# Decay sums unsplit in the fp32 stacks, decay rows in fewer partitions, later float32r stacks

## Chip, core and metric

The kernel runs on one core of a Trainium2 chip. The metric is the device time in microseconds (us) of one execution, median over several runs; less is better. Beside the time there is one profiled execution, from which all rows below come.

## What is computed

An attention with a decay, and two feed-forward layers over its output. In short:

```python
q, k, v: (4, 8, 576, 64)   f: (4, 8, 576)            # float32
cum = cumsum(log(clip(f, 1e-4, 1)), axis=-1)         # the decay sums
scores = q @ k^T / 8 + cum[:, :, :, None] - cum[:, :, None, :]   # masked causally
attn = softmax(scores) @ v                           # then (2304, 512)
h = x @ w1_in;  y = (h * tanh(softplus(h))) @ w1_out # 512 -> 2048 -> 512
h = y @ w2_in;  out = (h * cos(h)) @ w2_out          # 512 -> 2048 -> 512
```

The weights come as float64 and are split on the chip into two float32r parts (`split_weights`).

## The kernel before

**Attention.** `attention_units` works through jobs of two heads of one batch. Batch 0 (`CUT_BATCHES`) is cut into 8 jobs: four of the query blocks 0 and 1 (256 tokens), then four of the blocks 2 to 4. The batches 1 to 3 have four jobs each. `whole(jb)` is true for the 8 jobs of batch 0; the score products of these are plain fp32 (line 503), those of the other 12 jobs are sums of two float32r products (line 510).

**The stacks.** A score product takes its operands from a stack, a tile of 128 partitions whose rows 0 to 63 hold q or k, transposed. The decay enters the same product through more rows: where q has -1, k has cum of the key, and where k has 1, q has cum of the query. Before the change each cum stands as two rows, a float32r part hi and the rest lo (`cums`, `cumd`). They lie in partitions 64, 65 (k) and 96, 97 (q). `new_stack` (lines 652 to 660) fills the 32 partitions around them with four memsets: zeros in q[96:128] and k[64:96], always by GpSimd (lines 656, 657), then -1 and 1 (lines 658, 659) by the engine `en`. There are two fp32 stacks `stk0`, `stk1` and two float32r stacks `stkr0`, `stkr1`, used in turn by odd and even jobs. `stk0`, `stk1` and `stkr0` are made before the first job (lines 674 to 679), `stkr1` at its first use, in the place of the fp32 stacks.

**The start.** `decay_tables` loads f, clips it, takes Ln (ScalarE) and the running sum (VectorE scan, line 751), splits it into hi (ScalarE, line 753) and lo (VectorE, line 754). Then the jobs' loads are issued, and `prep_job(0)`: the row DMAs of job 0 from SBUF (line 426, four of them), the two writes of the sums to DRAM (`cumd`, line 434), transposes of q and k on TensorE (line 450) and the copies into the stack: of q the first head by VectorE (line 475), all the others by ScalarE (line 473). Later jobs read their rows from DRAM (line 428, two DMAs each). All DMAs are issued from SyncE's in-order queue.

**Per query block.** `scores` makes the products, a fused add of the mask with a minimum on VectorE (line 553, it reads `maskt` or `mask2`), exp on ScalarE (559); `normalise` scales on GpSimd (573); `transposes` (599, 610) and `av` (635) follow. `make_masks` fills the masks on GpSimd (lines 732 to 742).

**Beside it.** The weights of the first layer are converted piece by piece, one about every second query block: a load (105), two steps on VectorE (124, 125), a scaling on GpSimd (129), VectorE (134), ScalarE (138), GpSimd (139). Its first load is issued behind the write to DRAM marked `marks["cum"]`. After the first four jobs the products x @ w1_in of finished tokens (line 154) are put between the attention's steps; after the attention come the rest of both layers. Within these lists the order on each engine is made by a planner at build time (`schedule_with_timeline_sim=True`), which simulates the engines and issues, of what is ready, what comes first in the program; so instructions may stand in another order than in the text.

Of the kernel before, what the change touches and what calls it, by code (L numbers as in the profile page):

```python
# [9 lines left out]
F32 = mybir.dt.float32  # L10
F32R = mybir.dt.float32r
I32 = mybir.dt.int32
AF = mybir.ActivationFunctionType
ALU = mybir.AluOpType
# [18 lines left out]
def f(ap):  # L33
    return ap.bitcast(F32)
# [3 lines left out]
def tile_attention_two_ffn(  # L38
# [12 lines left out]
    nc = tc.nc  # L51
    B, H, S, D = q.shape
# [15 lines left out]
    dram = ctx.enter_context(tc.tile_pool(name="dram", bufs=1, space=DRAM))  # L68
# [8 lines left out]

    hd = dram.tile([128, NJ, NT], F32, name="hd")
    yd = dram.tile([128, 2, NK, NT], F32, name="yd")
    cumd = dram.tile([B * H, 2, S], F32, name="cumd")  # L80


# [3 lines left out]
    marks, cums = {}, []  # L86
# [268 lines left out]
    def attention_units(p, bank):  # L355
# [11 lines left out]
        def whole(jb):  # L367
            return jobs[jb][0] // NP in CUT_BATCHES
# [47 lines left out]
        def prep_job(jb):  # L416
            if jb >= len(jobs):
                return
            b, hp, qlo, khi, last = span(jb)
            qn, kn = nat.pop(jb)  # L420
            st = stack(jb)
            h0 = b * H + 2 * hp
            for row, x in ((96, 0), (64, 1)) if whole(jb) else ((96, 2), (64, 3)):
                if jb == 0:
                    for y in range(2):
                        nc.sync.dma_start(out=st[row + y : row + y + 1, x], in_=cums[y][h0 : h0 + 2])
                else:
                    nc.sync.dma_start(
                        out=st[row : row + 2, x] if whole(jb) else f(st[row : row + 2, x]),
                        in_=cumd[h0 : h0 + 2].rearrange("h y s -> y h s")  # L430
                    )
            if jb == 0:
                for y in range(2):
                    marks["cum"] = nc.sync.dma_start(out=cumd[:, y], in_=cums[y])
            yield
            cols = []
            for which, src, lo in ((0, qn, qlo), (1, kn, 0)):
                P, C = SPLIT[khi - lo]
                cols += [(which, src, P, C, c) for c in range(C)]
            full, groups = 512, []  # L440
            for x in cols:
                if full + x[2] > 512:
                    groups.append([])
                    full = 0
                groups[-1].append(x + (full,))
                full += x[2]
            for g in groups:
                t = bank()
                for which, src, P, C, c, at in g:
                    nc.tensor.transpose(t[:, at : at + P], src[0:P, c].rearrange("p h d -> p (h d)"), ident[0:P, 0:P])  # L450
                for which, lo in ((0, qlo), (1, 0)):
                    run = [x for x in g if x[0] == which]
                    if not run:
                        continue
                    _, _, P, C, c0, at = run[0]
                    n = len(run)
                    lo_x = 0 if which == 0 else 3
                    lo_r = slice(64, 128) if which == 0 else slice(0, 64)

                    def part(rows, x, j):  # L460
                        if jb == 0:
                            return st[rows, x, j, lo:khi].rearrange("r (p c) -> r c p", c=C)[:, c0 : c0 + n]
                        return st[rows, x, j, lo + c0 * P : lo + (c0 + n) * P]

                    sc = 0.125 if which == 0 else 1.0
                    if whole(jb):
                        for j in range(2):
                            i_ = t[64 * j : 64 * j + 64, at : at + n * P]
                            if jb == 0:
                                i_ = i_.rearrange("r (c p) -> r c p", p=P)  # L470
                            o = part(slice(0, 64), which, j)
                            if which or j:
                                nc.scalar.activation(out=o, in_=i_, func=AF.Copy, scale=sc)
                            else:
                                nc.vector.tensor_scalar(out=o, in0=i_, scalar1=sc, scalar2=None, op0=ALU.mult)
                        continue
                    for j in range(2):
                        i_ = t[64 * j : 64 * j + 64, at : at + n * P]
                        hi = part(slice(0, 64), which, j)
                        nc.scalar.activation(out=hi, in_=i_, func=AF.Copy, scale=sc)  # L480
                        nc.vector.scalar_tensor_tensor(
                            out=part(lo_r, lo_x, j), in0=i_, scalar=sc, in1=f(hi), op0=ALU.mult, op1=ALU.subtract
                        )
                    both = slice(0, 2)
                    dup = (slice(0, 64), 2) if which == 0 else (slice(64, 128), 1)
                    nc.gpsimd.tensor_copy(part(*dup, both), f(part(slice(0, 64), which, both)))
                yield
            if jb:
                load_v(jb + 1)
            load_job(jb + 2)  # L490

        def scores(jb, i):
            st = stack(jb)
# [6 lines left out]
            def product(o, j, c0, c1, first=QS[i], m=r):  # L500
                if whole(jb):
                    at = j * S + first
                    marks["score"] = nc.tensor.matmul(  # L503
                        o, lhsT=st.rearrange("p x j s -> p (x j s)")[0:128, at : at + m],
                        rhs=st[0:128, 1, j, c0:c1], start=True, stop=True,
                    )
                    return
                for x in range(2):
                    at = (4 * x + j) * S + first
                    marks["score"] = nc.tensor.matmul(  # L510
                        o, lhsT=st.rearrange("p x j s -> p (x j s)")[0:128, at : at + m],
                        rhs=st[0:128, 2 * x + 1, j, c0:c1], start=(x == 0), stop=(x == 1),
                    )

            heads = []
            if w == 64:
                t = bank()
# [3 lines left out]
                for j in range(2):  # L521
                    rows = slice(w * j, w * j + w)
                    heads[0].append((t[rows, w * j : w * j + w], 0, w, maskt[rows, S - 128 + w * j : S - 64 + w * j], rows))
            elif r == 64:
                t = bank()[:, 0:w]
# [6 lines left out]
            else:  # L532
                cuts = [(0, w)] if w <= 512 else [(0, w // 2), (w // 2, w)]
                heads = [[], []]
                for c0, c1 in cuts:
                    n = c1 - c0
                    t = None
                    for j in range(2):
                        if t is None or 2 * n > 512:
                            t = bank()  # L540
                        o = t[:, j * n : j * n + n] if 2 * n <= 512 else t[:, 0:n]
# [3 lines left out]
            for j, parts in enumerate(heads):  # L545
                s = p.tile([128, S], F32, tag="s", name="s", bufs=7)
# [105 lines left out]
        def new_stack(pool, name, dt, en):  # L652
            one = dt == F32
            t = pool.tile([128, 2 if one else 4, 2, S], dt, name=name, bufs=1)
            q, k = (t[:, 0], t[:, 1]) if one else (f(t[:, 2]), f(t[:, 3]))
            nc.gpsimd.memset(q[96:128], 0.0)
            nc.gpsimd.memset(k[64:96], 0.0)
            en.memset(q[64:96], -1.0)
            en.memset(k[96:128], 1.0)
            return t  # L660

        def stack(jb):
            key = (whole(jb), jb % 2)
            if key not in stacks:
                if key == (False, late % 2):
                    early.close()
                    pool = late_sb.enter_context(tc.tile_pool(name="stk", bufs=1))
                else:
                    pool = p
                stacks[key] = new_stack(pool, f"stkr{jb % 2}", F32R, nc.gpsimd)  # L670
            return stacks[key]
# [3 lines left out]
        for i in range(2):  # L675
            stacks[True, i] = new_stack(e, f"stk{i}", F32, nc.gpsimd if i else nc.vector)
            if i == 0:
                make_masks()
        stack(late - 1)
        for jb in range(2):  # L680
            load_job(jb)
        load_v(0)
        load_v(1)
        for _ in prep_job(0):
            pass
        prep = None
        M = len(items)
        LT = PAIR_LAG
# [55 lines left out]
    def decay_tables(p):  # L744
        NH = B * H
        ft, cum, one = (p.tile([128, S], F32, tag="s", name="s", bufs=7)[0:NH] for _ in range(3))
        nc.sync.dma_start(out=ft, in_=fg.rearrange("b h s -> (b h) s"))
        nc.vector.tensor_scalar(out=ft, in0=ft, scalar1=1e-4, scalar2=1.0, op0=ALU.max, op1=ALU.min)
        nc.scalar.activation(out=ft, in_=ft, func=AF.Ln)
        nc.gpsimd.memset(one, 1.0)  # L750
        nc.vector.tensor_tensor_scan(out=cum, data0=one, data1=ft, initial=0.0, op0=ALU.mult, op1=ALU.add)
        ch, cl = (x.bitcast(F32R) for x in (ft, one))
        nc.scalar.activation(out=ch, in_=cum, func=AF.Copy)
        nc.vector.tensor_tensor(out=cl, in0=cum, in1=ft, op=ALU.subtract)
        cums.extend((ft, one))

    hidden = [(0, 256), (256, S - 256)] + [(b * S + x, S // 2) for b in range(1, B) for x in (0, S // 2)]
    first = [(0, TH), (TH, TH), (2 * TH, NT % TH)] + [(NT - TH * i, TH) for i in (2, 1)]
# [137 lines left out]
```

## Time and profile before

| | us |
|---|---|
| median of 3 runs (1055.45 to 1059.02) | 1055.91 |
| profiled execution | 1053.56 |
| its span, first to last instruction | 1051.8 |
| TensorE busy in the span | 1011.2 |
| VectorE / ScalarE / GpSimd busy | 598.3 / 537.6 / 236.9 |

Engines in rows: PE is TensorE's matmul, PEld its weight load, DVE VectorE, ACT ScalarE, POOL GpSimd, SP SyncE; SPq is SyncE's queue, whose rows are the time an issue takes there. A name such as L503 is line 503 of the kernel. In a timeline the columns are start, duration (of all in the row), engine, line, operation, out<-in, shape, count, and in brackets the idle time before with what ended it. In a table of stretches each engine has its busy time and (count), then come the granted clock of TensorE as a share of full speed, the DMA engines' share, and GB/s.

### The profile page before, as it was taken

How to read it: one execution, taken by the hardware profiler on the slowest of the kernel's cores; microseconds unless marked ns; L12 is line 12 of the kernel's file. 1: busy time of each engine (PE TensorE's matmuls, PEld its weight loads, DVE VectorE, ACT ScalarE, POOL GpSimd, SP SyncE). 2: the span in 40 equal slices, each digit the busy share in tenths (PEclk: the TensorE clock that was granted, in tenths of full speed). 3: DMA queues.
4: the chain of work that ended last, by engine and by line, in shares of the span. 5: the costliest groups of instructions: out<-in, count | busy, mean ns of one | idle time of the engine just before them, and what ended most of it. 6: DMA issues, size and time to landing. Idle time of an engine off the chain costs nothing.

```text
span 1051.8 us, 16908 instructions
## 1 busy us (share of the span) xinstructions
PE 1011.2 (96%) x5920; PEld 865.8 (82%) x5920; DVE 598.3 (57%) x1402; ACT 537.6 (51%) x1142; POOL 236.9 (23%) x331
## 2 busy tenths in 40 slices
PE   5798899999999999999999999999999999999998
PEld 4586779899999999977778888888888888888897
DVE  5858755666555536746664267766444544454454
ACT  4666746665556536446664465644433333333343
POOL 7647643433323312412120012111000000000000
PEclk9999999999999999999999999999999999999999
DMA  4655423333331138756966365412100300110010
GB/s 118 169 151 123 136 70 95 85 93 89 84 90 60 57 117 277 238 176 196 325 206 223 111 195 177 159 41 71 50 1 1 120 1 1 41 41 1 1 41 21
DMA packets 118361, 111.80 MB, mean 106 GB/s; under 512 B 66564, under 2 KB 87044, under 8 KB 118276
## 3 DMA queue, kind: packets, MB, share of 16 engines
q1 hardware_dynamic: 118276, 110.72, 34.5%
q8 instruction: 47, 0.77, 0.3%
q14 instruction: 38, 0.31, 0.1%
HBM read 77.49 MB, written 33.18 MB: 105 GB/s over the span
## 4 chain that ended last, share of the span: by engine, by line
PE 77%; DMA 8%; DVE 5%; ACT 4%; issue 3%; POOL 3%; SPq 0%; ACTq 0%; POOLq 0%; DVEq 0%
PE h L154 24%; PE acc L257 19%; PE hx L154 9%; DMA hl<-hd 5%; PE s L635 5%; PE acc L249 5%; PE s L610 4%; PE s L510 3%; PE hx L249 2%; PE h L249 2%; PE s L450 2%; PE s L503 2%; DMA raw<-in_moe_w_in_dram 1%; POOL wol L139 1%; DVE gl L319 1%
## 5 line engine op out<-in xcount | busy, mean ns | idle before, releaser
L154 PE MATMUL h<-xb,wih 128*128 128x288 f32 (+2 forms) x848 | 184.2, 305 | 4.0 <-ACT wih L138 2.7
L154 PEld LDWEIGHTS h<-xb,wih 128*128 128x128 f32 x848 | 138.7, 191 | 7.1 <-ACT wih L138 3.2
L154 PE MATMUL h<-xb,wil 128*128 128x288 f32 (+2 forms) x424 | 126.3, 300 | 0.0
L559 ACT ACTIVATE s<-s,mx 128x448 f32<-128x448 f32 (+5 forms) x144 | 83.7, 582 | 68.4 <-DVE mx L553 64.4
L257 PE MATMUL acc<-woh,gh 128*128 128x512 f32 x288 | 112.9, 392 | 0.0
L257 PE MATMUL acc<-woh,gl 128*128 128x512 f32 x288 | 112.3, 391 | 0.0
L257 PE MATMUL acc<-wol,gh 128*128 128x512 f32 x288 | 112.0, 389 | 0.0
L573 POOL TENSOR_SCALAR s<-s,sm 128x448 f32<-128x448 f32 (+5 forms) x144 | 82.8, 588 | 124.4 <-DVE sm L571 63.4
L319 DVE TENSOR_TENSOR gl<-hl,gh 128x512 fp32r<-128x512 f32 x72 | 65.0, 904 | 70.5 <-ACT gh L314 70.4
L154 PE MATMUL hx<-x,wih 128*128 128x512 f32 (+1 forms) x320 | 92.7, 369 | 0.0
L154 PE MATMUL h<-x,wih 128*128 128x512 f32 (+1 forms) x320 | 91.0, 369 | 0.0
L305 ACT ACTIVATE n<-n 128x512 f32<-128x512 f32 (+1 forms) x80 | 47.1, 589 | 85.8 <-DVE n L299 85.6
L139 POOL TENSOR_TENSOR wol<-raw,woh 128x512 fp32r<-128x512 f32 x32 | 45.3, 1416 | 197.6 <-ACT woh L138 174.0
L553 DVE CUSTOM_DVE_ANT_0 s<-s,maskt 128x288 f32<-128x288 f32 (+6 forms) x152 | 63.7, 430 | 45.3 <-PE s L510 24.9
L319 DVE TENSOR_TENSOR gl<-e,gh 128x512 fp32r<-128x512 f32 (+1 forms) x80 | 53.8, 672 | 50.7 <-ACT gh L314 50.5
L154 PEld LDWEIGHTS h<-xb,wil 128*128 128x128 f32 x424 | 79.9, 190 | 1.3 <-issue 0.8
L298 DVE TENSOR_SCALAR n<-e 128x512 f32<-128x512 f32 (+1 forms) x80 | 32.7, 408 | 84.3 <-ACT e L291 83.8
L288 ACT ACTIVATE hl<-hl 128x512 f32<-128x512 f32 x72 | 45.1, 629 | 61.1 <-DMA hl<-hd 59.4
L314 ACT ACTIVATE gh<-e 128x512 fp32r<-128x512 f32 (+1 forms) x80 | 47.1, 588 | 52.3 <-DVE e L310 48.9
L249 PE MATMUL acc<-gl,woh 128*128 128x512 f32 (+1 forms) x192 | 68.5, 358 | 3.3 <-DVE gl L319 3.2
L249 PE MATMUL acc<-gh,wol 128*128 128x512 f32 (+1 forms) x192 | 67.8, 354 | 0.0
L154 PEld LDWEIGHTS h<-x,wih 128*128 128x128 f32 x320 | 58.4, 188 | 11.0
(119 smaller groups left out, 2215.7 us busy)
## 6 DMA issues: line engine op xcount, KB each, us to landing
hl<-hd SPq DMA_DIRECT2D x72, 256.0 KB
raw<-in_moe_w_in_dram SPq DMA_DIRECT2D x32, 512.0 KB
raw<-in_moe_w_out_dram SPq DMA_DIRECT2D x32, 512.0 KB
hd<-hs SPq DMA_DIRECT2D x48, 288.0 KB
yd<-stage SPq DMA_DIRECT2D x32, 256.0 KB
x<-yd SPq DMA_DIRECT2D x32, 256.0 KB
natk<-in_k_dram SPq DMA_DIRECT2D x32, 144.0 KB
out_dram<-stage SPq DMA_DIRECT2D x18, 256.0 KB
```

The source lines that it names most:

```text
L139: nc.gpsimd.tensor_tensor(out=lo[sl], in0=f(high), in1=f(hi[sl]), op=ALU.subtract)
L154: nc.tensor.matmul(o, lhsT=a[wsl], rhs=b[:, kk, :], start=(kk == 0 and i == 0), stop=(kk == NK - 1 and i == 2),)
L249: nc.tensor.matmul(acc[ti][d][:, 0:T], lhsT=a[dsl], rhs=b[:, gs], start=(start and i == 0), stop=(end and i == 2),)
L257: nc.tensor.matmul(acc[ti][m], lhsT=a[:, ms], rhs=b[:, j % 2, :], start=(start and i == 0), stop=(end and i == 2),)
L288: nc.scalar.activation(out=e, in_=e, func=AF.Mish, scale=UNSCALE)
L305: nc.scalar.activation(out=t, in_=t, func=AF.Sin, scale=TWO_PI)
L314: nc.scalar.activation(out=gh, in_=e, func=AF.Copy)
L319: marks["v1"] = nc.vector.tensor_tensor(out=gl, in0=st.pop(n)[0], in1=f(gst[n][0]), op=ALU.subtract)
L553: marks["ttr"] = nc.vector.tensor_tensor_reduce(out=s[rows, c0:c1], in0=o, in1=mk, scale=-1.0, scalar=BIG if prev is None or rows.start el ...
L559: nc.scalar.activation(out=s[:, 0:w], in_=s[:, 0:w], func=AF.Exp, scale=-1.0, bias=mx, accum_out=sm[:, j : j + 1])
L573: nc.gpsimd.tensor_scalar(out=s[:, 0:w], in0=s[:, 0:w], scalar1=sm[:, j : j + 1], scalar2=1.0, op0=ALU.mult, op1=ALU.mult)
L635: pair = nc.tensor.matmul(t[64 * j : 64 * j + 64, c0:width], lhsT=vt[jb][:, c, j], rhs=pt[:, j, c, c0:width], start=(c == 0), stop=(c == n ...
```

## The change

The fp32 stacks take cum itself, one row for k (partition 64) and one for q (partition 65), where hi and lo had been; a new DRAM tensor `cumf` holds it for later jobs. The float32r stacks keep hi and lo, now in partitions 64, 65 (k) and 66, 67 (q). `new_stack` has two memsets, both by `en`, over 2 or 4 partitions; the zero memsets are gone, and the products take 66 partitions (fp32) or 128 and 68 (float32r). The split into hi and lo and its two writes to DRAM come in `decay_parts`, behind `prep_job(0)`. `stkr0` is made at its first use, in `prep_job(8)`. Of job 0, VectorE copies both heads of q, and ScalarE both of k.

```diff
+    cumf = dram.tile([B * H, S], F32, name="cumf")
...
-            for row, x in ((96, 0), (64, 1)) if whole(jb) else ((96, 2), (64, 3)):
-                if jb == 0:
-                    for y in range(2):
-                        nc.sync.dma_start(out=st[row + y : row + y + 1, x], in_=cums[y][h0 : h0 + 2])
-                else:
+            if whole(jb):
+                for row, x in ((64, 1), (65, 0)):
                     nc.sync.dma_start(
-                        out=st[row : row + 2, x] if whole(jb) else f(st[row : row + 2, x]),
-                        in_=cumd[h0 : h0 + 2].rearrange("h y s -> y h s")
+                        out=st[row : row + 1, x], in_=cums[0][h0 : h0 + 2] if jb == 0 else cumf[h0 : h0 + 2]
+                    )
+            else:
+                for row, x in ((64, 3), (66, 2)):
+                    nc.sync.dma_start(
+                        out=f(st[row : row + 2, x]), in_=cumd[h0 : h0 + 2].rearrange("h y s -> y h s")
                     )
             if jb == 0:
-                for y in range(2):
-                    marks["cum"] = nc.sync.dma_start(out=cumd[:, y], in_=cums[y])
+                marks["cum"] = nc.sync.dma_start(out=cumf, in_=cums[0])
...
-                            if which or j:
+                            if which or j and jb:
...
-                        o, lhsT=st.rearrange("p x j s -> p (x j s)")[0:128, at : at + m],
-                        rhs=st[0:128, 1, j, c0:c1], start=True, stop=True,
+                        o, lhsT=st.rearrange("p x j s -> p (x j s)")[0:66, at : at + m],
+                        rhs=st[0:66, 1, j, c0:c1], start=True, stop=True,
...
-                for x in range(2):
+                for x, rows in ((0, 128), (1, 68)):
...
-            nc.gpsimd.memset(q[96:128], 0.0)
-            nc.gpsimd.memset(k[64:96], 0.0)
-            en.memset(q[64:96], -1.0)
-            en.memset(k[96:128], 1.0)
+            rows = slice(64, 66 if one else 68)
+            en.memset(q[rows], -1.0)
+            en.memset(k[rows], 1.0)
...
-        stack(late - 1)
...
         for _ in prep_job(0):
             pass
+        decay_parts()
...
-        ch, cl = (x.bitcast(F32R) for x in (ft, one))
-        nc.scalar.activation(out=ch, in_=cum, func=AF.Copy)
-        nc.vector.tensor_tensor(out=cl, in0=cum, in1=ft, op=ALU.subtract)
-        cums.extend((ft, one))
+        cums.extend((cum, ft, one))
+
+    def decay_parts():
+        cum, hi, lo = cums
+        nc.scalar.activation(out=hi.bitcast(F32R), in_=cum, func=AF.Copy)
+        nc.vector.tensor_tensor(out=lo.bitcast(F32R), in0=cum, in1=hi, op=ALU.subtract)
+        for y, t in enumerate((hi, lo)):
+            nc.sync.dma_start(out=cumd[:, y], in_=t)
```

## Rows read from the trace of the kernel before

**Rows 1.** Table of stretches, the whole span by stage.
```profile
0.00:50.00 50.00, 30.98 (x161) 21.98 (x162) 33.75 (x108) 30.14 (x82) 33.88 (x57) 0.99 0.61 150
...
80.00:143.00 63.00, 53.01 (x401) 42.67 (x399) 51.87 (x159) 43.44 (x113) 44.70 (x63) 0.95 0.46 118
...
200.00:400.00 200.00, 200.00 (x1602) 184.91 (x1602) 108.17 (x396) 112.80 (x303) 60.36 (x116) 1.00 0.31 89
```

**Rows 2.** Timeline of PE, 4 to 19 us.
```profile
11.56 1.20 PE L503 MATMUL s<-stk 128*128 128x128 f32 x4 [5.67 <-DMA stk<-s]
16.46 1.20 PE L503 MATMUL s<-stk 128*128 128x128 f32 x4 [0.66 <-DMA stk<-cumd]
```

**Rows 3.** Timeline of SP's queue, 7 to 15 us.
```profile
6.98 0.47 SPq L411 DMA_DIRECT2D natv<-in_v_dram  x1
7.58 2.73 SPq L426 DMA_DIRECT2D stk<-s  x4
10.37 0.86 SPq L434 DMA_DIRECT2D cumd<-s  x2
11.32 1.40 SPq L388 DMA_DIRECT2D natq<-in_q_dram  x2
...
14.24 0.68 SPq L428 DMA_DIRECT2D stk<-cumd  x2
```

**Rows 4.** Timelines of DVE and ACT, 0 to 15 us.
```profile
5.20 1.35 DVE L751 TENSOR_TENSOR_SCAN s<-s 32x576 f32<-32x576 f32 x1 [0.82 <-POOL mask L737]
6.48 0.58 DVE L475 TENSOR_SCALAR stk<-s 64x256 f32<-64x256 f32 x1
...
14.18 0.27 DVE L553 CUSTOM_DVE_ANT_0 s<-s,maskt 128x128 f32<-128x128 f32 x1
...
6.58 0.68 ACT L753 ACTIVATE s<-s 32x576 fp32r<-32x576 f32 x1 [1.49 <-DVE s L751]
7.29 1.90 ACT L473 ACTIVATE stk<-s 64x256 f32<-64x256 f32 x3
```

**Rows 5.** Timeline of POOL, 0 to 60 us.
```profile
1.53 1.06 POOL L656 MEMSET stk<- 32x1152 f32 x1
...
12.64 1.05 POOL L659 MEMSET stkr<- 32x1152 f32 x1
13.76 0.29 POOL L733 TENSOR_SCALAR_AFFINE_SELECT maskt<-maskt 128x128 f32<-128x128 f32 x1
```

**Rows 6.** Weight loads of all 128 rows and of 96, by shape, whole span.
```profile
L610 PEld LDWEIGHTS s<-ident,s 128*128 128x128 f32 x432 | 51.4, 145 | 3.4 <-DVE stkr L481 1.5 <-POOL s L573 1.0 <-issue 0.2
L450 PEld LDWEIGHTS s<-ident,natk 96*128 96x128 f32 x96 | 10.9, 146 | 0.2 <-issue 0.2
```

**Rows 7.** Timelines of POOL, DVE and PE around the making of stkr1.
```profile
98.30 1.05 POOL L659 MEMSET stkr<- 32x1152 f32 x1
99.44 0.71 POOL L129 TENSOR_SCALAR raw<-raw 128x512 f32<-128x512 f32 x1
...
94.73 0.43 DVE L124 TENSOR_SCALAR raw<-raw 128x512 int32<-128x512 int32 x1 [1.16 <-DMA raw<-in_moe_w_in_dram]
...
98.51 1.13 DVE L124 TENSOR_SCALAR raw<-raw 128x512 int32<-128x512 int32 x1
...
103.94 0.91 PE L635 MATMUL s<-p,natv 128*64 128x64 f32 x12 [2.58 <-DVE p L594]
```

**Rows 8.** Table of stretches, two in which the granted clock is at half.
```profile
104.00:110.00 6.00, 6.00 (x38) 5.88 (x39) 2.42 (x10) 4.19 (x12) 3.45 (x4) 0.50 0.33 100
50.00:54.00 4.00, 4.00 (x17) 3.59 (x18) 2.33 (x2) 0.86 (x2) 3.61 (x5) 0.50 0.18 32
```

**Rows 9.** Timelines of PE and of SP's queue, two single rows.
```profile
49.87 0.87 PE L599 MATMUL s<-ident,s 128*128 128x128 f32 x3 [4.15 <-DVE xb L648]
...
37.57 0.65 SPq L428 DMA_DIRECT2D stkr<-cumd  x2
```

**Rows 10.** Table of stretches, the four us around the start of stkr1's memsets.
```profile
92.00:96.00 4.00, 3.17 (x21) 2.56 (x20) 2.40 (x7) 1.76 (x5) 3.88 (x7) 1.00 0.94 288
```

More of the change, by code (lines that the diff above doesn't have):

```diff
@@ L503, in product @@
                     marks["score"] = nc.tensor.matmul(
-                        o, lhsT=st.rearrange("p x j s -> p (x j s)")[0:128, at : at + m],
-                        rhs=st[0:128, 1, j, c0:c1], start=True, stop=True,
+                        o, lhsT=st.rearrange("p x j s -> p (x j s)")[0:66, at : at + m],
+                        rhs=st[0:66, 1, j, c0:c1], start=True, stop=True,
                     )
                     return
-                for x in range(2):
+                for x, rows in ((0, 128), (1, 68)):
                     at = (4 * x + j) * S + first
                     marks["score"] = nc.tensor.matmul(
-                        o, lhsT=st.rearrange("p x j s -> p (x j s)")[0:128, at : at + m],
-                        rhs=st[0:128, 2 * x + 1, j, c0:c1], start=(x == 0), stop=(x == 1),
+                        o, lhsT=st.rearrange("p x j s -> p (x j s)")[0:rows, at : at + m],
+                        rhs=st[0:rows, 2 * x + 1, j, c0:c1], start=(x == 0), stop=(x == 1),
                     )
```

## The prediction

> **What bounds the kernel now.** I read the table of stretches first, then the timelines of the start, engine by engine, then the waits of PE. PE is busy 200 us of 200 between 200 and 400 us [rows 1], and nearly so to the end, so nothing that the change does to other engines can count there. Only two stages have room: the first 50 us, where PE works 30.98 us, and 80 to 143 us, where it idles 10 us [rows 1]. What is gained in them arrives at the end if the same instructions follow in the same order, since all later PE work is then simply started sooner.
>
> In the start PE first waits 5.67 us for the decay rows of job 0 [rows 2]. Those were the four issues on SP's queue from 7.58 to 10.31, and the last landed about 1.25 us after its issue (11.56 - 10.31) [rows 2, 3]. DVE's first masked minimum comes only at 14.18, 2 us after the first products [rows 2, 4]: it needs the mask, whose select stood behind all memsets of POOL and ran at 13.76 [rows 5]. The rows of job 1, issued at 14.24, are the next wall (PE at 16.46 waits for them) [rows 2, 3].
>
> **The change part by part.** The sum is made against the profiled execution, 1053.56 us with a span of 1051.8; the median is 2.35 us (0.2%) above it. I take differences and put them on the median, 1055.91.
>
> *First wall, rows of job 0.* cum is there when the scan ends, 5.20 + 1.35 = 6.55 [rows 4]. SP's queue is busy with loads of v until 6.98 + 0.47 = 7.45, which the planner finds ready and earlier in the program, so the first row issue stays at about 7.58 [rows 3]. Two issues in place of four cost 2.73 / 2 = 1.37 instead of 2.73: the last leaves at 8.95, lands at 10.2, and PE starts about 1.4 us sooner. If the v loads were passed, 0.9 us more. The copies don't hold it: ScalarE has two of 1.90 / 3 = 0.63 us, done by 7.29 + 1.27 = 8.56 even if they start no sooner than now; VectorE two of 0.58 from 6.48, done by 7.7 [rows 4].
>
> *Mask wall.* POOL loses eight of ten memsets of 1.05 us (two of stk0, two of stk1, four of stkr0) ahead of the select [rows 5], so the mask is ready before 8 and DVE starts when the first products are there, about 10.8 instead of 14.18: 3.4 us. That is the most that the start can gain.
>
> *Second wall, rows of job 1.* On SP's queue, from 7.58 to 14.24, stand four row issues (2.73), two writes (0.86) and four loads [rows 3]. After: two rows (1.37), one write of cumf (0.43), the loads, and the two moved writes of `decay_parts` (0.86), which come before job 1's rows in the program. Saved: 3.59 - 2.66 = 0.93 us; 1.8 if the moved writes slip behind. PE's second job, at 16.46, comes so much sooner. The split itself (0.68 on ScalarE [rows 4], a little more on VectorE) moves into time in which both idle until 14 us; without that cover it would cost about 1.4.
>
> So the start gains between 0.9 us (SP decides) and 3.4 (the mask decides). The next stage hangs on PE's and SP's walls and on DVE's, so I take a value nearer the lower end, 1.6. Late next is DVE, whose in-order queue carries both softmax and weight conversion.
>
> *Matmuls with 66 or 68 rows.* The trace has no such score product. A weight load of 96 rows takes 146 ns, one of 128 rows 145 [rows 6]: I take nothing. Bounds: 1 ns either way on each score load, and these are fewer than the 432 of the row: 0.4 us either way.
>
> *stkr1.* Two memsets fewer when it is made: POOL's L129 at 99.44, which follows the four directly, can start up to 2.1 us sooner [rows 7]. One DVE step beside the last memset, L124 at 98.51, takes 1.13 us instead of 0.43 [rows 7]. PE idles 2.58 us shortly behind, until 103.94 [rows 7]. Bounds 0 and 2.1 us; the chain runs through VectorE's and ScalarE's steps too, so I take 0.8.
>
> That DVE step is weighed against the Trainium skill: "SBUF — State Buffer", section "Who interferes with whom", says that VectorE's two-port forms and a GpSimd instruction exclude each other for a whole instruction. The row agrees (1.13 against 0.43); by the rule the memsets put at a new place cost VectorE up to their full length there, 2.1 us for two, which would eat the 0.8 and 1.3 more. It speaks against the later stkr0.
>
> *stkr0 at its first use.* Two memsets of 1.05 us move from the start to `prep_job(8)`, ahead of that job's row issues, which SP reached at 37.57 [rows 9], long before job 8 computes. I expect the planner to put them into one of POOL's free spells before 50 us (16 us are free there [rows 1]): cost 0; bound 2.1 if in the way.
>
> Sum: -1.6 - 0.8 + 0 = -2.4, so 1055.91 - 2.4 = 1053.5. Bounds: -0.9 + 2.1 = +1.2 and -3.4 - 2.1 = -5.5.
>
> **The rivals.** *A stretch of slow clock goes too.* The granted clock is 0.95 to 1.00 on average in the stages [rows 1] (2.4 GHz is the full level), but 0.50 (1.2 GHz) in 50 to 54 and in 104 to 110 us [rows 8], after PE had idled 4.15 us before 49.87 [rows 9] and 2.58 us before 103.94 [rows 7]. PE is busy in all of the second stretch, so it loses half of 6 us, 3 us. If the relieved POOL shortens that idle time, the 3 us come on top: 1053.5 - 3.0 = 1050.5; with the larger memset gain (2.1) 1049.2; if the first gap also closes (half of 4 us), 1047.2. For it: four memsets stand just there. Against it: PE waits for DVE there, and the first gap hangs on a weight load and on a change of PSUM pools, which the change leaves alone. The Trainium skill, "TensorE: Matmul & The Clock Gate", section "Loop structure matters more than you think", says that waits between matmuls make the array slow; the trace agrees, with 0.50 behind both gaps.
>
> *The gain is lost at the next wall.* Loads and weight pieces are paced by buffers and by POOL's and DVE's steps; if these decide from 20 us on, a start 1 to 3 us sooner ends in a longer wait. Time 1055 to 1056. Against it: the first load of the weight pieces also waits for the write of the sums and so comes earlier too. That the change misses its aim (the fewer DMAs don't land sooner) ends here as well.
>
> *Slower: stkr0's memsets come into the way.* If the planner puts them where job 8 is prepared (85 us and later), POOL has no room (3.88 of 4 us busy [rows 10]); the casts and scalings wait 2.1 us, and job 8's row DMAs wait on SP's in-order queue with the weight loads behind them, up to another 2.1 us. PE's gap before 103.94 grows by as much and the slow clock behind it by some 3 us. With the start's gain: -1.6 + 2.1 to 4.2 + 3 = +3.5 to +5.6, so 1059.4 to 1061.5. It decides the result from the point where the memsets begin later than about 85 us. A new order of the planner that opens another such gap elsewhere has the same price.
>
> **How the numbers follow.** Forecast (gain of 1 to 5 us) 0.42; slow clock also gone 0.31; gain lost 0.12; slower 0.15. Predicted 1053.5. The range 1047.0 to 1059.5 leaves out about 2 in 10: the far part of the slower case, and a little below. About 0.5% (5.3 us) is what a measurement of this kernel tells from no change: faster means below 1050.6, most of the clock case (0.27) and the forecast's outer end (0.04): 0.31. Slower, above 1061.2, is the far half of the slower case, 0.08, with the chance of two such gaps in it. The same: 0.61.
>
> **What would show it.** Right: two row issues at about 7.6, PE's first score product near 10.2, first DVE minimum before 11.5, the mask's select before 8, job 1's products near 15.3, two memsets for stkr1, PE's table of stretches the same but shifted by 1 to 3 us from 50 us on, and stkr0's memsets before 50 us. Wrong: a first product still after 11, stkr0's memsets after 85, or another count and place of the half-clock stretches; these would move the time by more than the start does.

## The result and the profile after

The changed kernel takes 1061.1 us, median of 14 runs (1057.21 to 1067.58), against 1055.78 us (1053.46 to 1059.02) of the kernel before beside it: ratio 1.0052 (95% interval 1.0034 to 1.0069). It is slower by 5.3 us where 2.4 us less was forecast, and lies outside the range. Here and below each ratio is against the kernel before, run beside it (its median lay between 1055.78 and 1057.32 us). The profiled execution took 1061.13 us with a span of 1059.3. That of before (1053.56) is 2.2 us under its own median, so of the 7.5 us between the two traces about 2 are chance.

The start went as worked out. The timeline of SP's queue in the changed kernel, columns as in the rows of before:

```profile
7.57 1.41 SPq L426 DMA_DIRECT2D stk<-s  x2
...
12.36 1.01 SPq L759 DMA_DIRECT2D cumd<-s  x2
13.47 0.51 SPq L426 DMA_DIRECT2D stk<-cumf  x2
```

Its timeline of PE:

```profile
10.23 1.19 PE L504 MATMUL s<-stk 66*128 66x128 f32 x4 [4.29 <-DMA stk<-s]
15.40 1.19 PE L504 MATMUL s<-stk 66*128 66x128 f32 x4 [0.94 <-DVE mx L554]
```

Of DVE:

```profile
11.57 0.29 DVE L554 CUSTOM_DVE_ANT_0 s<-s,maskt 128x128 f32<-128x128 f32 x1 [3.56 <-PE s L504]
```

Of POOL:

```profile
4.99 1.05 POOL L658 MEMSET stkr<- 4x1152 f32 x1
5.99 1.05 POOL L659 MEMSET stkr<- 4x1152 f32 x1
7.11 0.29 POOL L733 TENSOR_SCALAR_AFFINE_SELECT maskt<-maskt 128x128 f32<-128x128 f32 x1
```

PE begins its first score product 1.33 us sooner and job 1 1.06 us sooner [rows 2]. The loss comes later. Where the start of the same PE instruction stands in the two traces (after less before, median by stage):

| stage of before, us | 10-20 | 20-30 | 35-40 | 45-50 | 55-95 | 110-115 | 140-400 | from 480 |
|---|---|---|---|---|---|---|---|---|
| shift, us | -1.3 | -0.8 | +3.2 | +9.4 | +5.4 | +3.1 | +5.8 to +6.3 | +7.5 |

The step between 400 and 480 us stands at a half-clock stretch (449.0 to 452.4 us in the changed kernel) that this trace of the kernel before does not have, but nine of the ten other traces of the whole computation do, four variants of the kernel before among them, so it cannot be put down to the change. What has to be explained lies between 30 and 55 us. PE's timeline there, first of before:

```profile
29.19 0.69 PE L610 MATMUL s<-ident,s 128*128 128x128 f32 x2
...
31.75 1.28 PE L503 MATMUL s<-stk 128*128 128x256 f32 x6
...
36.89 0.76 PE L503 MATMUL s<-stk 128*64 128x320 f32 x4 [2.36 <-ACT stk L473]
...
38.08 1.67 PE L503 MATMUL s<-stk 128*128 128x448 f32 x4
...
41.53 2.13 PE L503 MATMUL s<-stk 128*128 128x288 f32 x8
...
44.85 0.87 PE L635 MATMUL s<-p,natv 128*64 128x256 f32 x8
```

and of the changed kernel:

```profile
28.37 0.69 PE L611 MATMUL s<-ident,s 128*128 128x128 f32 x2
...
41.31 3.19 PE L504 MATMUL s<-stk 66*128 66x448 f32 x4
44.44 1.55 PE L636 MATMUL s<-p,natv 128*64 128x256 f32 x8
...
47.89 4.10 PE L504 MATMUL s<-stk 66*128 66x288 f32 x8
...
53.90 1.49 PE L636 MATMUL s<-p,natv 128*64 128x256 f32 x8
56.42 0.88 PE L600 MATMUL s<-ident,s 128*128 128x128 f32 x3 [1.03 <-DVE xb L649]
...
59.66 1.75 PE L504 MATMUL s<-stk 66*128 66x448 f32 x4
```

The same four products of 448 columns take 1.67 us before and 3.19 after, eight of 288 columns 2.13 and 4.10, and `av`, which the change does not touch, 0.87 and 1.55. Everything on PE is twice as long: its clock stands at 1.2 GHz until about 59.8 us, where it rose to 2.4 GHz at about 31.7 before. From the transposes that start at 29.19 or 28.37 to the end of `av` at 45.72 or 55.39, PE works 14.2 us before (16.53 less a rest of 2.36) and 24.1 after (27.02 less rests of 1.52 and 1.43): 9.9 us more for the same work. The rest that follows, 4.15 us in [rows 9], is 1.03 now, and before fell to half clock behind it [rows 8]; that gives back some 4, and +5.4 us remain.

The granted-clock column doesn't show this. In the table of stretches the changed kernel has

```profile
0.00:50.00 50.00, 35.43 (x141) 24.37 (x142) 30.78 (x94) 27.08 (x73) 28.00 (x48) 1.00 0.55 136
40.00:50.00 10.00, 10.00 (x35) 6.21 (x34) 5.88 (x18) 5.77 (x14) 4.83 (x8) 1.00 0.39 100
80.00:143.00 63.00, 54.44 (x417) 42.07 (x415) 49.10 (x151) 42.82 (x114) 39.75 (x57) 0.95 0.51 134
138.00:142.00 4.00, 3.77 (x16) 2.30 (x18) 3.66 (x15) 3.70 (x12) 1.74 (x4) 0.57 0.35 80
200.00:400.00 200.00, 199.41 (x1601) 183.83 (x1599) 109.38 (x411) 113.01 (x308) 61.01 (x117) 1.00 0.30 84
```

It stands at 1.00 up to the first change of clock that the trace holds, and is right only behind it. Ahead of it the durations tell the level. I read the 0.99 of [rows 1] as full speed, and it was not. In 40 to 50 us PE is busy without a break and the clock still stays low.

### The profile page after: what moved, and what is told of

It reads as the page before. It is cut to its first block, busy times and chain, and to the rows that moved or that the text cites. A ratio compares the mean times of both kernels' runs of the same rounds, so it can differ in the third digit from the quotient of the medians.

```text
span 1059.3 us, 16904 instructions
## 1 busy us (share of the span) xinstructions
PE 1023.1 (97%) x5920; PEld 871.3 (82%) x5920; DVE 598.3 (56%) x1403; ACT 537.6 (51%) x1141; POOL 227.4 (21%) x323
## 4 chain that ended last, share of the span: by engine, by line
PE 46%; DMA 2%; DVE 1%; ACT 1%; issue 1%; POOL 0%; ACTq 0%; DVEq 0%
PE acc L258 19%; PE hx L155 9%; PE h L155 9%; PE acc L250 5%; PE hx L250 2%; PE h L250 2%; DMA hl<-hd 1%; DMA raw<-in_moe_w_in_dram 0%; DVE gl L320 0%; DMA yd<-stage 0%; ACT gh L315 0%; DVE raw L126 0%; ACT hl L289 0%; DVE raw L125 0%; POOL wil L140 0%
## 5 line engine op out<-in xcount | busy, mean ns | idle before, releaser
L554 DVE CUSTOM_DVE_ANT_0 s<-s,maskt 128x288 f32<-128x288 f32 (+6 forms) x152 | 64.0, 432 | 48.7 <-PE s L511 22.5
L320 DVE TENSOR_TENSOR gl<-e,gh 128x512 fp32r<-128x512 f32 (+1 forms) x80 | 53.3, 667 | 50.7 <-ACT gh L315 50.5
L315 ACT ACTIVATE gh<-e 128x512 fp32r<-128x512 f32 (+1 forms) x80 | 47.1, 588 | 52.5 <-DVE e L311 49.5
L636 PE MATMUL s<-p,natv 128*64 128x256 f32 (+3 forms) x544 | 62.9, 373 | 5.3 <-ACT p L593 3.1
```

The costliest lines, as they stand in the source:

```text
L315: nc.scalar.activation(out=gh, in_=e, func=AF.Copy)
L320: marks["v1"] = nc.vector.tensor_tensor(out=gl, in0=st.pop(n)[0], in1=f(gst[n][0]), op=ALU.subtract)
L554: marks["ttr"] = nc.vector.tensor_tensor_reduce(out=s[rows, c0:c1], in0=o, in1=mk, scale=-1.0, scalar=BIG if prev is None or rows.start el ...
L636: pair = nc.tensor.matmul(t[64 * j : 64 * j + 64, c0:width], lhsT=vt[jb][:, c, j], rhs=pt[:, j, c, c0:width], start=(c == 0), stop=(c == n ...
```

## The experiments

**Theory.** Products over 66 partitions keep TensorE's clock down longer than the same products over 128; each takes as long as before at either level, but all of PE's work stays at half speed until the rise. **Rivals.** The planner's new order moved PE's rests, and the clock follows these; or the 66 rows cost time by themselves at full clock, or it is the float32r products over 68.

**Rows alone, in the kernel before.** Two kernels, 66 or 98 partitions in place of 128. With 66 the query's cum (partitions 96, 97) is left out, a constant in each softmax row.

```diff
-                        o, lhsT=...[0:128, at : at + m],
-                        rhs=st[0:128, 1, j, c0:c1], start=True, stop=True,
+                        o, lhsT=...[0:66, at : at + m],
+                        rhs=st[0:66, 1, j, c0:c1], start=True, stop=True,
```

> The kernel before, but its fp32 score products take 66 partitions instead of 128; memsets, DMAs and the split sums stay. It leaves out the cum of the query, which is the same for a whole row of the softmax. Theory (rows): products over 66 partitions leave the TensorE clock at half; matmul durations stay at the doubled values (score products of 256 columns above 500 ns) until 50 us or later, where the kernel before has full-speed durations from 31.5 us; time 4 to 8 us above the kernel before. Rival (order): what counts is the planner's new order and its idle gaps; this kernel has nearly the order of before, so full speed from about 31 us and a time within 2 us of before.

> The kernel before with 98 partitions in the fp32 score products (all rows that carry the decay; only empty rows are left out). On TensorE, VectorE, ScalarE and GpSimd the instructions stand in the same order as with 66. Theory (rows): between the two, full speed earlier than with 66, at best as early as before, time 0 to 4 us above before. Rival (order): as with 66, since the order is the same: the same time as that run.

Measured: 66 rows 1060.06 us, ratio 1.0018 (1.0000 to 1.0037); 98 rows 1057.72, ratio 1.0001 (0.9985 to 1.0018). The planner gives both the same order on PE, VectorE, ScalarE and GpSimd, only SyncE's queue differs a little. On PE it is also the order of the changed kernel for the first 526 matmul records, up to 109 us. PE's timeline with 66 rows:

```profile
40.46 3.19 PE L503 MATMUL s<-stk 66*128 66x448 f32 x4
47.04 4.10 PE L503 MATMUL s<-stk 66*128 66x288 f32 x8
```

and with 98:

```profile
39.12 3.19 PE L503 MATMUL s<-stk 98*128 98x448 f32 x4
44.59 2.13 PE L503 MATMUL s<-stk 98*128 98x288 f32 x8
```

Both have a first spell at full clock from about 30 us. With 98 the clock is back at 43.3, ahead of the products of 288 columns, with 66 only at 54.6: in one order of PE's work, 98 rows in place of 66 bring it back 11 us sooner. The times show less. With 66 rows the 4 to 8 us of the rows theory did not come (1.9 us by the ratio), the difference of the two, 2.3 us, is less than the 5.3 of the change, and the intervals overlap.

**All 128 rows, in the changed kernel.** The unused rows are zero or meet zeros; first the fp32 products, then the second float32r product too.

```diff
-                        o, lhsT=...[0:66, at : at + m],
-                        rhs=st[0:66, 1, j, c0:c1], start=True, stop=True,
+                        o, lhsT=...[0:128, at : at + m],
+                        rhs=st[0:128, 1, j, c0:c1], start=True, stop=True,
...
+            if one:
+                nc.gpsimd.memset(k[64:128], 0.0)
+                en.memset(q[64:128], -1.0)
```

> The changed kernel, with its fp32 products over 128 partitions again (one zero memset and a fuller -1 memset per fp32 stack; the float32r products keep 68). Theory (rows): the clock rises at about 30 us as in the kernel before, and the gain of the start (1.1 us at the first products) is kept: time 1 to 3 us below before, 6 to 8 below the change. Rival (order): durations stay doubled until 55 to 60 us, time 4 to 6 us above before.

> As the run before it, and the second float32r products take 128 partitions too. Theory (rows): after 60 us other matmuls over all rows keep the clock up, so the 68 rows cost nothing: within 2 us of the run with 128 in the fp32 products alone. If the 68 rows matter in 95 to 160 us: 2 to 4 us faster than that run. Rival (order): 4 to 6 us above before.

Measured: 1058.95 us, ratio 1.0012 (0.9996 to 1.0029), and 1059.91, ratio 1.0019 (1.0003 to 1.0034). With the fp32 rows goes the greater part of the loss (1.0052 against 1.0012), with the float32r rows nothing that shows. The clock rises at about 28.6 us, earlier than before. PE's order is the changed kernel's until about 28 us; behind that 432 of 5920 matmul records stand in other places, so a part of the 4 us may be the order's. The 1 to 3 us below before that the rows theory gave did not come: what is left of the gain of the start is lost behind rests:

```profile
36.07 1.33 PE L504 MATMUL s<-stk 128*64 128x320 f32 x4 [2.30 <-DMA stk<-cumf]
...
38.24 3.19 PE L504 MATMUL s<-stk 128*128 128x448 f32 x4
...
43.66 2.13 PE L504 MATMUL s<-stk 128*128 128x288 f32 x8
...
52.20 0.57 PE L600 MATMUL s<-ident,s 128*128 128x128 f32 x3 [3.82 <-DVE sm L572]
```

Behind the rest of 2.30 us the products are slow again (3.19 for four of 448 columns), until 42 us; behind that of 3.82 once more. The first rival has a share, then. The length of the rest alone does not decide: the kernel before rests 2.36 us ahead of the same products (36.89 above) and stays at full clock.

**Rows by themselves.** Nothing of the reference is computed: six stretches of 24 groups, each group three fp32 products of 128x256 and ScalarE's copy of the result, on which the next group waits.

```diff
+    for rows in (66, 128, 66, 128, 98, 34):
+        for _ in range(24):
+            for _ in range(3):
+                nc.tensor.matmul(t[:, 0:256], lhsT=st[0:rows, 0:128], rhs=st[0:rows, 256:512], ...)
+            nc.scalar.activation(out=st[:, 0:128], in_=t[:, 0:128], func=AF.Copy)
```

> Nothing of the reference is computed here: TensorE alone runs six stretches of 24 groups of three fp32 products of 128x256, each group waiting for ScalarE's copy of the one before, with some 10 us of rest ahead of each stretch. The contracted rows are 66, 128, 66, 128, 98 and 34 in this order. Rows theory (products over fewer rows hold the clock down): the stretches over 128 rows reach products of 0.43 us each early, those over 66 later or never (0.8 us each), so a stretch of 66 rows is 10 to 25 us longer than one of 128; 98 lies between, 34 is slowest. Rival (rows don't matter to the clock, the order of work does): the stretches after the first are equally long within 2 us, with the rise at the same place of each.

The rests of 10 us ahead of the stretches fell away (0.77 us), so the stretches follow each other directly. PE's timeline, changes of stretch and the last group:

```profile
93.80 2.93 PE L40 MATMUL t<-st 66*128 66x256 f32 x6 [0.43 <-ACT st L41]
97.50 2.93 PE L40 MATMUL t<-st 128*128 128x256 f32 x6 [0.77 <-ACT st L36]
101.31 1.56 PE L40 MATMUL t<-st 128*128 128x256 f32 x6 [0.89 <-ACT st L41]
104.98 1.56 PE L40 MATMUL t<-st 128*128 128x256 f32 x6 [2.11 <-ACT st L41]
...
150.77 1.56 PE L40 MATMUL t<-st 66*128 66x256 f32 x6 [0.77 <-ACT st L36]
154.58 1.87 PE L40 MATMUL t<-st 66*128 66x256 f32 x6 [2.25 <-ACT st L41]
158.25 2.93 PE L40 MATMUL t<-st 66*128 66x256 f32 x6 [1.80 <-ACT st L41]
...
228.99 2.93 PE L40 MATMUL t<-st 66*128 66x256 f32 x6 [0.43 <-ACT st L41]
...
249.50 1.56 PE L40 MATMUL t<-st 128*128 128x256 f32 x6 [0.43 <-ACT st L41]
...
295.12 2.93 PE L40 MATMUL t<-st 98*128 98x256 f32 x6 [1.48 <-ACT st L41]
...
446.66 2.93 PE L40 MATMUL t<-st 34*128 34x256 f32 x6 [0.43 <-ACT st L41]
```

Stretches of its table, the third (66 rows), the fourth (128) and the fifth (98):

```profile
160.00:228.00 68.00, 59.15 (x123) 37.32 (x122) 0.00 (x0) 7.13 (x21) 0.00 (x0) 0.50 0.00 0
250.00:285.00 35.00, 27.62 (x107) 18.57 (x106) 0.00 (x0) 4.74 (x18) 0.00 (x0) 1.00 0.00 1
295.00:365.00 70.00, 61.03 (x126) 38.78 (x126) 0.00 (x0) 9.00 (x22) 0.00 (x0) 0.50 0.00 0
```

Here no order can be blamed. The first stretch over 66 rows runs all its 24 groups at half clock, the third all from its third group on, though PE is busy 59.15 us of 68; over 128 rows the clock rises after 3.6 us in the second stretch and after 15.2 in the fourth, and stays up though PE is busy for a smaller share (27.62 of 35). Behind the change back to 66 rows it falls after 4.9 us, behind that to 98 after 4.6, and over 34 it stays down. The first groups of a stretch also wait longer, for the copies on ScalarE that were to make the rests (2.25 us at 154.58). So the rows are not all that changed at the fall; but over 128 rows two such waits of 2.11 us (at 104.98 and 108.65) did not bring the clock down, and later, in an even rhythm, it does not come back over 66 or 98 rows. The rival's "equally long within 2 us" fails: from the first group of a stretch to that of the next it is 81.9, 53.3, 81.9, 54.9 and 81.9 us for 66, 128, 66, 128 and 98 rows. Of the theory's own forecast, the 10 to 25 us between 66 and 128 rows were passed (27 to 29), and 98 does not lie between nor is 34 slowest: all three stay down alike.

The Trainium skill, "TensorE: Matmul & The Clock Gate", section "LDWEIGHTS (loading the stationary operand)", says that a weight load takes its time by the columns and not by the contracted rows. The rows agree: at half clock a weight load takes 324 to 328 ns on average with 34, 66, 98 and 128 rows. The products don't depend on the rows either (2.93 us for a group with each of the four at half clock). So the forecast's "nothing" was right for one product, and the clock was left out.

**More work for PE.** If the clock is the cause, useless work that keeps PE busy with 128 rows should bring the rise forward. In the changed kernel and in the kernel before:

```diff
+            if jb < 8:
+                t = bank()
+                for _ in range(3):
+                    nc.tensor.matmul(t[:, 0:256], lhsT=ss[1][:, 0:128], rhs=wr, start=True, stop=True)
...
+        for _ in range(2):
+            nc.tensor.matmul(t[:, 0:256], lhsT=wr[:, 0:128], rhs=wr, start=True, stop=True)
```

> The changed kernel, plus two fp32 products of 128x256 at the start and three more in the transposes of each query block of jobs 0 to 7; their results are read by nobody, and the whole result is computed. Clock theory (the kernel loses because TensorE stays on the half clock until 59.8 us of the trace): the added work brings the rise to full clock ahead of 45 us, the products of 448 columns at 40 us come out near 0.45 us each instead of 0.8, and the time falls below that of the changed kernel by 2 to 6 us, to 1055 to 1059 us. Rival (the order of the work, not the clock, costs the time; added work is added time): the 26 added products or so, at 0.43 to 0.8 us each, make it 5 to 15 us longer, 1066 us or more.

> The kernel before, with the same added products whose results nobody reads. Clock theory: the half-clock stretches of the kernel before at 0 to 32 us and at 48.7 to 55.6 us become shorter by 5 to 15 us in all, which is worth at most 0.4 us each, so 1052 to 1056 us, no longer than before in spite of the added work. Rival (added work is added time): 1061 to 1070 us.

> The changed kernel unaltered, beside the others on the same chip: 1059 to 1063 us, 0.3 to 0.7 per cent above the kernel before, by every theory.

Measured: 1062.96 us, ratio 1.0066 (1.0051 to 1.0081); 1062.68, ratio 1.0060 (1.0045 to 1.0075); the changed kernel again 1061.74, ratio 1.0053 (1.0032 to 1.0075), its clock rising at 59.5 us. Neither fill gave the clock theory's time: the first lies between the two forecasts, the second in the rival's range. In both the added work also costs time of its own, as the rows below show. With the first the clock does rise early, at 24.6 us, and the products of 448 columns take 1.67 us, as over 128 rows. A row of PE's timeline, and the group of the added products in the table of lines (count | busy us, mean ns of one | idle):

```profile
39.69 1.67 PE L504 MATMUL s<-stk 66*128 66x448 f32 x4
```

```profile
L624 PE MATMUL s<-wr,s 128*128 128x256 f32 x96 | 25.1, 398 | 0.0
```

The shift against before is +0.7 us at 55 to 60 us (+5.4 without the fill), but it grows to +6 and more by 140: nearly half of the 25.1 us of added work stands after 60 us, where PE has no room. With the second, in the kernel before, the memset of the fill's operand stood behind GpSimd's memsets and PE waited for it, so the whole start came 4.3 us later (its timeline of PE):

```profile
14.14 2.07 PE L694 MATMUL s<-wr 128*128 128x256 f32 x4 [8.27 <-POOL wr L691]
```

**Work only in the rests.** So the last three have useless 128x128 products only where PE rests anyway: three before the first score product, six behind the transposes at 34 us, fourteen behind the last `av` at 49 us. The first is the changed kernel with 128 rows, the second the kernel before, the third the changed kernel with 66 rows.

```diff
+            if (jb, i) == (2, 0):
+                for _ in range(6):
+                    nc.tensor.matmul(t[:, 0:128], lhsT=ss[1][:, 0:128], rhs=ident, ...)
...
+            if jb == 3:
+                for _ in range(14):
+                    nc.tensor.matmul(t2[:, 0:128], lhsT=pt[:, 0, 0, 0:128], rhs=ident, ...)
...
+        for _ in range(3):
+            nc.tensor.matmul(t[:, 0:128], lhsT=ident, rhs=ident, start=True, stop=True)
```

> The changed kernel with its fp32 products over all 128 partitions (unused rows set to zero once), plus useless 128x128 fp32 products in TensorE's three long rests of the first 55 us: three before the first score product, six after the transposes of the first query block of job 2 (the rest of 2.3 us at 33.8 us) and fourteen after the last product of job 3 (the rest of 3.8 us at 48.4 us). The whole result is computed. Clock theory: the half-clock stretches at 35 to 42 us and 52 to 56 us, each of which began right after such a rest, are gone, so the time falls by 2 to 4 us below the same kernel without them (1.0012 of the kernel before): ratio 0.996 to 0.999, 1052 to 1055 us. Rival (half clock there is beside waits that end no sooner, or the added products hold up the real ones): ratio 1.001 or more.

> The kernel before with the same useless products in the same three rests. Clock theory: its half-clock stretch at 48.7 to 55.6 us, behind the rest of 4.15 us, is gone, which gives back 2 to 3 us: ratio 0.997 to 0.999. Rival: no gain, ratio 1.000 or more.

> As the first of the three, but with the fp32 products over 66 partitions again. Rows theory: TensorE's clock rises later than with 128 rows, at 35 us or after, and the useless products make up only a part: 2 to 4 us more than with 128 rows, ratio 1.000 to 1.004. Rival (with the rests filled the number of rows makes no difference): the same time as the first within 1 us.

Measured: 1056.3 us, ratio 0.9989 (0.9975 to 1.0004); 1056.37, ratio 0.9987 (0.9970 to 1.0005); 1058.49, ratio 1.0010 (0.9992 to 1.0029). In the first, PE's timeline:

```profile
34.09 1.50 PE L627 MATMUL s<-ident,s 128*128 128x128 f32 x12
...
38.28 1.67 PE L507 MATMUL s<-stk 128*128 128x448 f32 x4
...
49.18 3.39 PE L653 MATMUL s<-ident,p 128*128 128x128 f32 x28
52.67 0.52 PE L603 MATMUL s<-ident,s 128*128 128x128 f32 x3
```

Its table of stretches:

```profile
30.00:60.00 30.00, 23.82 (x181) 18.05 (x179) 20.98 (x69) 17.60 (x47) 16.96 (x28) 1.00 0.71 176
```

The clock rises at 29.1 us and no half-clock stretch follows until 104 us: the one at 35 to 42 and the one at 52 to 56 are gone, with PE's other instructions in the same order around them. Filling the rests is worth about 2.4 us (1.0012 to 0.9989, each against before), and 2.2 us lie between 66 and 128 rows with the rests filled; in both pairs the intervals overlap a little. No kernel here is surely faster than before; the two with 128 rows are the nearest to it, by some 0.1%, and the first beats the changed kernel by 0.6%. But between these two themselves nothing is left of the change's gain: 1056.3 us against 1056.37. The Trainium skill, "TensorE: Matmul & The Clock Gate", section "HAM oscillation — how this bites in real kernels", says that waits for data between matmuls take the clock down. The half-clock stretches behind the rests of 2.30 and 3.82 us, and their absence with the fills, agree; the 2.36 us of the kernel before, with no such stretch behind, is a case that it does not settle.

The half-clock stretches by the trace, up to 160 us:

| kernel | half clock up to | and again |
|---|---|---|
| before | 31.7 | 48.7-55.6, 103.4-110.2 |
| changed | 59.8 | 104.2-107.6, 138.3-141.7 |
| changed, again | 59.5 | 103.8-110.7 |
| before, 66 rows | 30.7 | 34.1-54.6, 102.3-109.2, 129.6-133.1, 150.1-153.5 |
| before, 98 rows | 29.6 | 36.5-43.3, 97.9-101.3, 142.3-145.7 |
| changed, 128 rows | 28.6 | 35.5-42.3, 52.5-55.9, 100.3-103.7, 120.8-131.0 |
| changed, 66 rows, rests filled | 39.3 | 97.3-104.2, 124.6-128.1 |
| changed, 128 rows, rests filled | 29.1 | 104.2-107.6 |
| before, rests filled | 29.1 | 117.9-124.7 |

## Why the prediction was wrong

**First wall: right.** Two issues from 7.57 us, 1.41 us long, first product at 10.23 (forecast 10.2). VectorE's and ScalarE's copies didn't hold it.

**Mask wall: right.** The select ran at 7.11 us, DVE's first minimum at 11.57 (10.8 was forecast): it waited for PE, no longer for the mask. POOL lost six memsets ahead of the select, not eight: stkr0's two stayed there.

**Second wall: the time right.** Job 1's products came at 15.40 (15.3), its rows' issues 0.77 us sooner (13.47 for 14.24 in [rows 3]); but the wait that ended last there was for DVE (0.94 us), no longer for the rows.

**Matmuls with 66 or 68 rows: here it failed.** "I take nothing", with 0.4 us either way from the weight loads of [rows 6], priced one instruction at one clock. What the rows bear on is which clock the whole engine gets. The term measures about +4 us in this kernel (1.0052 against 1.0012) and +2 in the kernel before or with the rests filled. A bound from the price of single instructions could not reach it; the nearest rows for that, the doubled durations at 12 to 31 us in the timeline of before, I had not read as half clock.

**stkr1: a gain that did not stay.** POOL's timeline there:

```profile
100.34 1.05 POOL L658 MEMSET stkr<- 4x1152 f32 x1
101.33 1.34 POOL L659 MEMSET stkr<- 4x1152 f32 x1
```

Two memsets, as said, each as long over 4 partitions as over 32. PE's rests between 95 and 105 us are 1.92 and 0.85 us, where before had 0.83, 0.86 and the 2.58 of [rows 7], and the half-clock stretch behind them lasts 3.4 us in place of 6.8 [rows 8]. The shift falls from +5.4 to +3.1, more than the 0.8 put there, and a new half-clock stretch at 138.3, the 0.57 in the table of stretches above, takes it back (+5.8). Neither is firm: in the second trace of the same kernel the stretch behind the rests lasts 6.8 us as before, the shift falls by just 0.8 (+5.1 to +4.3), and none follows at 138.

**stkr0: right in its cost.** Its memsets ran at 4.99 and 5.99 us, still ahead of the mask's select, and in nobody's way.

**The rivals.** The slow one named stkr0's memsets, which did nothing; its last sentence, a gap opened elsewhere by a new order, has the nearer mechanism: behind the rests of the changed kernel with 128 rows stand half-clock stretches that are gone with the rests filled. "The gain is lost at the next wall", named with 0.12, has a share too. With 128 rows and the rests filled in both, the clock is nearly even up to 400 us, and the changed kernel is no faster (1056.3 against 1056.37): its trace is 1.1 us ahead at 10 to 20 us and 0.7 us behind at 140 to 400, and between 40 and 49 us PE waits 0.73, 0.63 and 1.40 us for ScalarE where the kernel before with the fills does not wait. So the gain of 1.6 us that the forecast took from the start did not arrive at the end either. "A stretch of slow clock goes too" had the right resource and the wrong sign: 28 us of half clock came instead. It looked at two later stretches and took the start for full speed.

What stays open: why the same 66 rows cost some 4 us in the changed kernel and 2 in the other two, though PE's order is the same up to 109 us in the kernel before with 66; how much of the shift behind 100 us is chance, since two traces of the changed kernel differ there by up to 2 us; and whether fewer than 128 rows, more than 98, would do.

## What to carry to other kernels

Before you cut the contracted rows of a product to save memsets or DMAs, ask which clock TensorE has there, and read it from the durations: at the head of a trace the clock column can stand at 1.00 while every product takes twice its time. Zero rows up to 128 cost PE nothing per product here, and with them the clock rose at 28.6 us in place of 59.8. In rests of some 2 to 4 us between bursts a few useless products were nearly free; where PE has no room, added products cost their full length.

## What was not expected of the hardware

fp32 products over 66, 98 or 34 partitions, PE busy 59 to 61 us of 68 to 70, stayed at 1.2 GHz for whole stretches; where those over 66 and 98 followed products over 128, with a rest of 2.25 us ahead of the second group, the clock was down from 2.4 GHz within 5 us and did not come back. Over 128 it rose and stayed, with two rests of 2.11 us behind the rise, and in the kernel it rose with zeros in the rows from 66 on as well. At either level the duration of a product didn't depend on the rows.
